# Another written-out order for the first stage of a fused attention, MLP and expert kernel

## Chip, cores, metric

One core of a Trainium2 chip. The metric is the time of one execution on the device in microseconds (us); the kernel before takes 545.9 us (median of three runs, 545.31 to 547.83).

## What is computed

Three layers follow each other on 1536 tokens (2 x 768) of width 512 (8 heads x 64). All inputs come as float64, are read by the kernel as pairs of 32-bit words, or, for q, k, v, as float32.

```python
scores = scale * np.matmul(q_c, k_full.transpose(0, 1, 3, 2))   # chunks of 32 queries, 64 keys
a = np.exp(scores - np.max(scores, axis=-1, keepdims=True))
out[:, :, c_start:c_end] = np.matmul(a / (np.sum(a, axis=-1, keepdims=True) + 1e-09), v_full)
...
h = x @ w_in                                                    # 512 -> 2048
g = np.where(h > 0.0, h, np.exp(np.minimum(h, 0.0)) - 1.0)
x = g @ w_out                                                   # 2048 -> 512
...
expert_idx = np.argmax(x @ w_gate, axis=1)                      # 8 experts, capacity 384
...
h = np.maximum(np.einsum('ecd,edf->ecf', disp, w1), 0.0)
y = np.einsum('ecf,efd->ecd', h, w2)
out[i] = gate_w[i] * y[expert_idx[i], pos[i]]
```

## The kernel before

The tokens are cut into six tiles of 256 (called tile or pair 0 to 5), the middle layer's 2048 columns into sixteen units of 128. A step is two (unit, tile) pairs. Steps 0 to 3 take units 0 to 3 on tiles 0 and 1, steps 4 to 15 one unit each on both tiles, steps 16 to 47 two units each on tiles 2 to 5. The first stage, steps 0 to 15 and what goes with them, is emitted from a table of words, `ORDER` (L33 to L36): `do` reads one word after the other and emits that piece, so the table is at once the order of TensorE's, VectorE's, ScalarE's, GpSimd's and the load queue's own instructions. [...] A word is two letters and an index:

- Loads on the queue of SyncE: `lk`, `lq`, `lv` for k, q, v of a tile's half (`lq01` is tile 0, half 1; 512 KB, 256 KB, 512 KB), `lu` for both weight halves of a unit (`lu10`: unit 10, 2 x 512 KB).
- Attention of a tile's half: `sc` scores (L170, TensorE), `tm` and `ts` their maximum (VectorE), `ex` the exponentials (eight ScalarE instructions with sums, or one), `to` the reciprocal of the sum (VectorE), `di` the division (GpSimd), `fl` four transposes (L239, TensorE), `fc` their copy (ScalarE), `av` the product with the values (L255, TensorE), `xh` its rounded part (L270, ScalarE), `xl` the remainder (L274, VectorE). Both make up the tile's `xt`.
- A unit's weights from words to floats: `ca` (L358, ScalarE), `cb`, `cc`, `cd` (L378, L382, L391, VectorE); then rounded part and remainder of the first half (`ch`, `cl`) and of the second (`dh`, `dl`): L403 on ScalarE and L407 on VectorE.
- A step: `ma` first product (L465, 24 matmuls), `mr` three ScalarE instructions (L479 to L481), `mv` two on VectorE (L485, L491), `mh` and `ml` rounded part and remainder (L495, L499), `mb` second product (L520). Steps 0 to 5 skip `mh` and `ml` and take the unrounded weights in `mb`.
- `pm`, a filler product on the identity matrix (L456), which computes nothing that is used.

A star puts a word's instruction on VectorE instead of ScalarE or GpSimd, a plus puts it on GpSimd instead of VectorE.

Buffers tie the queues. Nineteen buffers of 8 KB hold the units' raw words, the split weights and `xt`; the load of a later unit waits until an earlier unit's raw words are done with, which is after its `dl`. The two accumulators of `ma` alternate, so `ma` of a step waits for `mv` of the step two before. Six more PSUM buffers serve the rest.

From step 16 on a loop emits one step at a time: `ma` of two steps ahead, a piece of background work, `mr`, `mv`, `mh`, `ml` of that step, another piece, `mb`, a third piece. Which pieces stands in `PLANS` (L26 to L31), one row per tile from tile 2 on: 16 entries for 8 steps, where A is attention of the next tile, R and S routing of an earlier one; what stands behind the bar comes after `mr` to `ml` and ahead of `mb`. Routing of tiles 0 to 4 adds up eight gate values on VectorE (L552), takes the maximum (L584 to L590), and has TensorE count places (L595 to L601).

Of the kernel before, what the change touches and what calls it, by code (L numbers as in the profile page):

```python
# [30 lines left out]
)  # L31

ORDER = """  # L33
lq00 lk00 pm pm pm pm sc00 tm00 ts00 ex00 lu0 cb0 to00 ca0 lq01 cc0 lk01 pm pm pm pm pm sc01 tm01 ts01 lu1 ca1 di00 pm pm fl00 cd0 fc00 cb1 cc1 cd1 ex01 to01 lk10 lq10 lv00 pm sc10 av00 ch0 ch1 lu2 tm10 di01 cb2 lk11 xh00 xl00 ca2 pm pm fl01 fc01 lv01 pm pm av01 lq11 ts10 cl1+ cc2 cd2 lu3 ex10 lq20 to10 lk20 xh01 xl01 lv11 sc11 tm11 ts11 ch2 ca3 cb3 cc3 cl0+ pm ma0 lv10 lu4 sc20 lu5 lu6 di10 fl10 cl2+ ex11 to11 di11* cd3 ch3* tm20 pm pm pm fl11 fc10 pm av10 xh10* fc11 mr0 mv0 av11 xh11 xl11 lq21 cl3+ cb4 ca4 cc4 cd4 xl10 ma1 lu7 mb0 mr1 mv1 ch4 cl4+ ca6 cb6 cc6 cd6 ma2 mr2 mv2 lu8 ts20 ch6 cl6+ lk21 mb1 mb2 ma3 lu9 cb7 cb9 cb5 ca7 dh6 dl6 ex20 ca5 lu10 ca10 cc7 cd7 ca8 mr3 cc5 cd5 dh0* mv3 sc21 ma4 dl0+ to20 di20 mb3 ch5 cl5 cb8 dh1 dl1 mr4 ca9 cc9 mv4 ch7 dh2 dl2+ cb10 cl7 ma5 cd9 mr5 dh7 cc8 mv5 mb4 dh4 lu11 tm21 ca11 cd8 dl4 lu12 ca12 cc10 ma6 mr6 mv6 ch9 dh9 dh3 dl3 mh6 dl7+ mb5 dh5* lv20 cl9+ ts21 ex21 ml6+ ch8* dh8 to21 cl8+ lu13 dl8 ma7 mr7 mv7 mb6 ma8 fl20 ma9 dl5+ cb11 mh7 mr8 cd10 ch10 cb12 ml7 mb7 dl9 mv8 mh8 ml8+ mb8 cl10 ma10 cc11 cd11 mr9 mv9 lv21 lu14 dh10 dl10+ lu15 ca15 ch11 cl11 mh9 ml9 cc12 cd12 mb9 fc20 ma11 mr10 mv10 mh10 ml10 di21 mb10 fl21 ch12 dh12 cl12 ma12 dl12 cb13 dh11 dl11 ca13 cc13 cd13 mr11 mv11 ch13 cl13 fc21 mh11 ml11 ca14 cb14 cc14 av20 xh20 xl20 dh13 dl13+ mb11 cd14 ch14* mr12 dh14 mv12 mh12 ml12 cb15 cc15 av21 xh21 ma13 mr13 mv13 mh13 cl14+ ma14 xl21 mr14 dl14+ mb12 ml13 mb13 cd15 ch15* cl15+ mv14 mh14 ma15 ml14 mb14 dh15 dl15 mr15 mv15 mh15 ml15 ma16 mr16 mv16 mh16 ml16+ mb15 ma17 mr17 mv17 mh17 ml17 lw lz0 lz1 lz2 lz3 lz4 lz5 lz6 lz7 lz8 lz9 lz10 lz11
"""


# [1190 lines left out]
```

## Time and profile before

| | us |
|---|---|
| median of three runs | 545.9 |
| the profiled execution's own time | 546.62 |
| its span in the trace | 544.9 |
| TensorE busy | 522.4 |
| VectorE busy | 347.4 |
| ScalarE busy | 292.9 |
| GpSimd busy | 124.3 |

The span is the time from the first to the last instruction in the trace; the 1.7 us between it and the execution's time lie around it. TensorE has work in 96% of the span, and the other engines are well below that as a mean. The mean hides the first 120 us, in which all sixteen units are converted and split: there VectorE has work nine tenths of the time. TensorE's share also counts the fillers (42 records, two to a word, 14.0 us), all in the first 32 us.

### The profile page before, as it was taken

The page shows a single profiled execution, that of the slowest core. Times are in us where ns is not written, and L with a number is a line of the kernel's source. Part 1 is how long each engine was busy: PE and PEld are TensorE (multiplying, and loading weights), DVE is VectorE, ACT ScalarE, POOL GpSimd, SP SyncE. Part 2 cuts the span into 40 slices and gives each one's busy share as a digit, 9 for nine tenths or more (in the row PEclk, how much of TensorE's full clock was granted, in tenths as well). Part 3 has the DMA queues.
Part 4 walks back from the last instruction along what each step waited for, and adds up shares of the span by engine and source line. Part 5 has one row for each costly group of instructions (what it writes and reads, how often), then busy time and mean ns, then how long its engine had stood idle before and what let it go on. Part 6 is the DMA issues. An engine that isn't in the chain of part 4 may idle for free. (4 is left out here: it accounts for less than half of the span.)

```text
span 544.9 us, 11455 instructions
## 1 busy us (share of the span) xinstructions
PE 522.4 (96%) x4520; PEld 448.0 (82%) x4520; DVE 347.4 (64%) x651; ACT 292.9 (54%) x569; POOL 124.3 (23%) x140
## 2 busy tenths in 40 slices
PE   7899999999999999999999999999999998999995
PEld 5766678988998888998888997878887886889894
DVE  5888989984456333787766996442685764674550
ACT  3877776764546447444545356242665655654441
POOL 2411354031123313124312324221001011010101
PEclk9899999999999999999999999899999998999999
DMA  8994349994004305431004562529539929905000
GB/s 342 402 413 198 131 177 281 265 352 154 1 21 136 118 2 194 155 134 61 3 2 155 211 235 96 193 96 379 175 118 353 396 79 380 362 28 193 20 7 26
DMA packets 34726, 95.94 MB, mean 176 GB/s; under 512 B 3424, under 2 KB 3424, under 8 KB 33888
## 3 DMA queue, kind: packets, MB, share of 16 engines
q1 hardware_dynamic: 32496, 88.68, 45.9%
q0 software_dynamic: 2160, 6.31, 3.0%
q8 instruction: 46, 0.75, 0.6%
q14 instruction: 24, 0.20, 0.1%
HBM read 88.67 MB, written 16.55 MB: 193 GB/s over the span
## 5 line engine op out<-in xcount | busy, mean ns | idle before, releaser
L465 PE MATMUL hp<-xt,un 128*128 128x256 f32 x1152 | 149.7, 286 | 1.3 <-ACT xt L270 0.6
L465 PEld LDWEIGHTS hp<-xt,un 128*128 128x128 f32 x1152 | 142.9, 191 | 7.3 <-issue 2.4
L520 PE MATMUL ps<-un,gt 128*128 128x512 f32 x504 | 125.5, 397 | 1.4 <-POOL gt L499 1.3
L520 PEld LDWEIGHTS ps<-un,gt 128*128 128x128 f32 x504 | 91.6, 188 | 22.1 <-POOL gt L499 2.4
L707 DVE TENSOR_TENSOR eu<-eraw,eu 128x1024 fp32r<-128x1024 f32 x65 | 77.3, 1225 | 19.5 <-ACT eu L706 12.9
L830 PE MATMUL ps<-eu,ht 128*128 128x512 f32 x336 | 82.6, 398 | 1.0 <-DVE eu L707 0.8
L830 PEld LDWEIGHTS ps<-eu,ht 128*128 128x128 f32 x336 | 61.8, 188 | 15.2 <-DVE eu L707 1.6
L499 POOL TENSOR_TENSOR gt<-th,gt 128x512 fp32r<-128x512 f32 x33 | 45.8, 1387 | 124.5 <-ACT gt L495 124.5
L485 DVE SCALAR_TENSOR_TENSOR th<-e,th 128x512 f32<-128x512 f32 x48 | 34.6, 722 | 51.9 <-ACT e L481 51.7
L706 ACT CAST eu<-eraw 128x1024 fp32r<-128x1024 f32 x65 | 65.2, 1046 | 0.7 <-ACT os L836 0.7
L495 ACT CAST gt<-th 128x512 fp32r<-128x512 f32 x42 | 26.1, 620 | 73.5 <-DVE th L491 73.5
L767 PE MATMUL hp<-xd,eu 128*128 128x256 f32 x480 | 59.1, 284 | 3.0 <-DVE eu L707 2.1
L767 PEld LDWEIGHTS hp<-xd,eu 128*128 128x128 f32 x480 | 58.1, 192 | 4.4 <-DVE eu L707 2.5
L479 ACT ACTIVATE e<-hp 128x512 f32<-128x512 f32 x48 | 28.8, 600 | 36.5 <-PE hp L465 34.8
L837 POOL DMA_INDIRECT out_dram<-os,meta x14 | 13.8, 983 | 138.0 <-ACT os L836 133.4
L407 POOL TENSOR_TENSOR un<-raw,un 128x512 fp32r<-128x512 f32 x16 | 23.9, 1500 | 54.6 <-ACT un L403 38.3
L792 PE MATMUL hq<-eu,xd 128*128 128x512 f32 x120 | 33.4, 427 | 2.4 <-issue 2.0
L753 DVE SCALAR_TENSOR_TENSOR ht<-hp,ht 128x512 fp32r<-128x512 f32 x20 | 13.8, 689 | 33.3 <-ACT ht L752 33.3
L480 ACT ACTIVATE th<-e 128x512 f32<-128x512 f32 x48 | 30.4, 632 | 5.6 <-DVE junk L552 3.0
L491 DVE SCALAR_TENSOR_TENSOR th<-hp,th 128x512 f32<-128x512 f32 x42 | 29.0, 691 | 4.0 <-DVE th L485 0.5
L481 ACT ACTIVATE e<-e 128x512 f32<-128x512 f32 x48 | 30.4, 632 | 1.5
L836 ACT ACTIVATE os<-ps,meta 128x512 f32<-128x512 f32 x14 | 9.6, 688 | 38.8 <-PE ps L830 28.5
(157 smaller groups left out, 594.0 us busy)
## 6 DMA issues: line engine op xcount, KB each, us to landing
eraw<-in_moe_w_dram SPq DMA_DIRECT2D x32, 1024.0 KB, 7.6
raw<-in_moe_w_in_dram SPq DMA_DIRECT2D x15, 512.0 KB, 7.6
raw<-in_moe_w_out_dram SPq DMA_DIRECT2D x15, 512.0 KB, 8.2
disp<-in_blank_dram SPq DMA_DIRECT2D x12, 514.0 KB, 14.8
kt<-in_k_dram SPq DMA_DIRECT2D x12, 512.0 KB, 6.8
v<-in_v_dram SPq DMA_DIRECT2D x12, 512.0 KB, 5.4
wb<-in_gate_rows_dram SPq DMA_DIRECT2D x6, 1024.0 KB, 4.6
xg<-disp SPq DMA_DIRECT2D x8, 514.0 KB, 9.5
```

The costliest lines, as they stand in the source:

```text
L465: nc.tensor.matmul(hp[:, j, :], units[f].un[:, 0, wp, kk * P : (kk + 1) * P], xts[ti][:, xp, kk, :], start=(n == 0), stop=(n == 3 * KD - 1),)
L480: nc.scalar.activation(th, e, AF.Tanh, scale=0.5)
L481: nc.scalar.activation(e, e, AF.Exp, scale=-1.0)
L485: nc.vector.scalar_tensor_tensor(out=th, in0=e, scalar=1.0, in1=th, op0=ALU.add, op1=ALU.mult)
L491: nc.vector.scalar_tensor_tensor(out=to, in0=hv, scalar=0.0, in1=th0, op0=ALU.max, op1=ALU.subtract)
L499: eng.tensor_tensor(out=gt[:, 1, :], in0=th, in1=f32(gt[:, 0, :]), op=ALU.subtract)
L520: nc.tensor.matmul(accs[ti][bl], x, w, start=(f == 0 and n == 0), stop=(f == NF - 1 and n == len(passes) - 1),)
L706: nc.scalar.copy(un[:, 0, :], raw)
L707: lows.tensor_tensor(out=un[:, 1, :], in0=raw, in1=f32(un[:, 0, :]), op=ALU.subtract)
L767: nc.tensor.matmul(hp[:, j, :], w1p(kk, wp, f * P, P), xd[xp][:, kk, :], start=(n == 0), stop=(n == 3 * KD - 1),)
L792: nc.tensor.matmul(hp, self.xd[xp][:, kk, self.b0 * P : (self.b0 + 1) * P], w1p(kk, wp, i * 512, 512), start=(n == 0), stop=(n == 3 * KD - 1),
L830: nc.tensor.matmul(acc, hof(f, gp, j), w2p(f, wp), start=(f == 0 and n == 0), stop=(f == NFE - 1 and n == 2))
```

## The change

The table `ORDER` is written anew; the words are the same 356, 21 fillers among them, but 34 of them change their engine, and nearly all their place in the order. Two rows of `PLANS` move a piece of attention and four pieces of routing. The program is otherwise the same.

```diff
 PLANS = (
-    "RR - A|S R RS SAA - RAA S SAA - A| - - - -",
-    "A A A ARA - ARAR RR| - |AR - - R RR R RR| R",
+    "RR - A|S R RS SAA - RAA S SAA |A - - - - -",
+    "A A A ARA - ARAR RR| - |AR R R R R - RR| R",
...
-lq00 lk00 pm pm pm pm sc00 tm00 ts00 ex00 lu0 cb0 to00 ca0 lq01 cc0 lk01 pm pm pm pm pm sc01
...
+lk00 lq00 pm pm pm pm sc00 tm00 ts00 ex00 lu0 lq01 cb0 to00 lk01 ca0 cc0 cd0 pm pm pm pm pm pm sc01
...
```

By word, the engines change so: VectorE gets one more `cl`, three more `dl`, three `fc` and one `di`, and gives up two `ch` and two `ml`, four instructions more in all. GpSimd loses one `di`, one `cl`, three `dl` and gets two `ml`. ScalarE loses three `fc` and gets two `ch`.

TensorE from the last filler ahead of the first product (`hp_112`, step 0) on, before; `ps_525` and `ps_554` are the transposes of tile 1, `gt_607` is step 0 after `mv`:

```order
L456 MATMUL hp_112<-ident 128x256
L465 MATMUL hp_112<-xt_283,un_318 128x256 x12
L465 MATMUL hp_112<-xt_283,un_320 128x256 x12
...
L239 MATMUL ps_525<-ident,a_391 128x128 x4
L456 MATMUL hp_550<-ident 128x256 x3
L239 MATMUL ps_554<-ident,a_531 128x128 x4
L456 MATMUL hp_550<-ident 128x256
...
L465 MATMUL hp_550<-xt_283,un_449 128x256 x12
L465 MATMUL hp_550<-xt_283,un_545 128x256 x12
L520 MATMUL ps_682<-raw_158,gt_607 128x512
```

And with the change:

```order
L456 MATMUL hp_112<-ident 128x256
L239 MATMUL ps_449<-ident,a_299 128x128 x4
L465 MATMUL hp_112<-xt_314,un_269 128x256 x12
L465 MATMUL hp_112<-xt_314,un_441 128x256 x12
L239 MATMUL ps_502<-ident,a_485 128x128 x4
...
L520 MATMUL ps_612<-raw_158,gt_552 128x512
...
L465 MATMUL hp_626<-xt_314,un_549 128x256 x12
L465 MATMUL hp_626<-xt_314,un_555 128x256 x12
L465 MATMUL hp_658<-xt_507,un_269 128x256 x12
```

Between `ma0` and `mb0` stand now one transpose group and the two values products (left out here as "..."), and neither a filler nor `ma1`; the four fillers that stood there are ahead of `ma0`, and `ma1` and `ma2` come after `mb0`.

VectorE with the change, around `mv5` (`gt_909`), `mv6` (`hp_913`) and `ml6` (`gt_960`); `raw_455` is unit 3, `raw_941` unit 10, `raw_949` unit 11:

```order
L407 TENSOR_TENSOR un_555<-raw_455,un_555 128x512
L485 SCALAR_TENSOR_TENSOR th_887<-e_886,th_887 128x512
L491 SCALAR_TENSOR_TENSOR gt_909<-hp_861,th_887 128x512
L407 TENSOR_TENSOR un_893<-raw_618,un_893 128x512 x2
L378 TENSOR_SCALAR raw_941<-raw_941 128x1024
L407 TENSOR_TENSOR un_895<-raw_621,un_895 128x512
L485 SCALAR_TENSOR_TENSOR th_954<-e_953,th_954 128x512
L491 SCALAR_TENSOR_TENSOR th_954<-hp_913,th_954 128x512
L378 TENSOR_SCALAR raw_949<-raw_949 128x1024
L407 TENSOR_TENSOR un_725<-raw_597,un_725 128x512
L499 TENSOR_TENSOR gt_960<-th_954,gt_960 128x512
```

Units 10 and 11 are loaded into buffers that earlier units leave: unit 10's load waits for VectorE, TensorE and ScalarE, unit 11's for VectorE, TensorE and GpSimd, and the last `dl` on VectorE ahead of them in the table is the first row here, `dl3`, and `dl7`, the second of the two `un_893`. Before, unit 10 still had a buffer of its own, and the first load that waited was unit 11's. The conversion of the two new units (`raw_941`, `raw_949`) stands ahead of `mv6` and `ml6`.

VectorE in tile 3, the routing of tile 2 (`lg_2636`), before and with the change; `hp_2893`, `hp_2943` and `hp_2896`, `hp_2949` are the accumulators of two steps in a row:

```order
L485 SCALAR_TENSOR_TENSOR th_2919<-e_2918,th_2919 128x512
L491 SCALAR_TENSOR_TENSOR th_2919<-hp_2893,th_2919 128x512
L552 SCALAR_TENSOR_TENSOR junk_2940,lg_2636<-x_268_2431,wb_2780 128x512
...
L485 SCALAR_TENSOR_TENSOR th_2975<-e_2974,th_2975 128x512
L491 SCALAR_TENSOR_TENSOR th_2975<-hp_2943,th_2975 128x512
L584 MAX rmx_2996<-lg_2636 128x8 x2
L586 MAX_INDEX rix_2997<-rmx_2996,lg_2636 128x8 x2
...
L590 TENSOR_SCALAR oh_2999<-iota_e,idf_2998 128x8 x2
```

```order
L485 SCALAR_TENSOR_TENSOR th_2925<-e_2924,th_2925 128x512
L491 SCALAR_TENSOR_TENSOR th_2925<-hp_2896,th_2925 128x512
L552 SCALAR_TENSOR_TENSOR junk_2946,lg_2636<-x_268_2431,wb_2780 128x512
...
L584 MAX rmx_2974<-lg_2636 128x8 x2
L586 MAX_INDEX rix_2975<-rmx_2974,lg_2636 128x8 x2
...
L590 TENSOR_SCALAR oh_2977<-iota_e,idf_2976 128x8 x2
L485 SCALAR_TENSOR_TENSOR th_2992<-e_2991,th_2992 128x512
L491 SCALAR_TENSOR_TENSOR th_2992<-hp_2949,th_2992 128x512
```

Four of the eight gate-value instructions that stood between the two `mv` have moved ahead of the first, and the maximum and the one-hot rows (`oh`) ahead of the second.

## Rows read from the trace of the kernel before

**Rows 1.** The page: span, busy time and instructions of each engine.

```profile
span 544.9 us, 11455 instructions
PE 522.4 (96%) x4520; PEld 448.0 (82%) x4520; DVE 347.4 (64%) x651; ACT 292.9 (54%) x569; POOL 124.3 (23%) x140
```

**Rows 2.** Busy time by stretch: length, engines (instructions), granted clock, DMA share, GB/s.

```profile
0.00:24.20 24.20, 18.95 (x426) 14.74 (x426) 15.08 (x28) 13.08 (x45) 7.29 (x16) 0.93 0.95 373
24.20:40.90 16.70, 15.46 (x267) 12.23 (x265) 14.86 (x27) 11.74 (x32) 4.01 (x4) 1.00 1.02 405
40.90:71.60 30.70, 30.57 (x218) 21.21 (x217) 28.00 (x37) 22.35 (x44) 8.75 (x6) 1.00 0.46 173
71.60:140.00 68.40, 67.28 (x531) 58.37 (x530) 54.88 (x77) 41.69 (x71) 17.57 (x14) 1.00 0.76 232
```

**Rows 3.** Timeline of TensorE: start, length, instructions, idle before and its releaser.

```profile
24.76 3.02 PE L465 MATMUL hp<-xt,un 128*128 128x256 f32 x23 [0.16 <-DVE xt L274]
27.71 0.86 PE L170 MATMUL ps<-kt,q 64*32 64x64 f32 x64
...
28.99 1.46 PE L456 MATMUL hp<-ident 128*128 128x256 f32 x6
...
33.77 1.02 PE L255 MATMUL ps<-at,v 64*64 64x32 f32 x56 [0.64 <-issue]
34.72 3.14 PE L465 MATMUL hp<-xt,un 128*128 128x256 f32 x24
37.70 3.77 PE L520 MATMUL ps<-raw,gt 128*128 128x512 f32 x8
40.87 3.46 PE L465 MATMUL hp<-xt,un 128*128 128x256 f32 x24
44.17 7.56 PE L520 MATMUL ps<-raw,gt 128*128 128x512 f32 x16
```

**Rows 4.** Timeline of the load queue, and issue to landing of single loads.

```profile
11.18 0.43 SPq L141 DMA_DIRECT2D v<-in_v_dram  x1
...
v<-in_v_dram SPq DMA_DIRECT2D x1, 512.0 KB, 10.2
...
raw<-in_moe_w_out_dram SPq DMA_DIRECT2D x1, 512.0 KB, 4.4
```

**Rows 5.** Timeline of ScalarE and VectorE around `mr2` and `mv2`.

```profile
44.37 0.60 ACT L479 ACTIVATE e<-hp 128x512 f32<-128x512 f32 x1 [2.89 <-PE hp L465]
...
46.32 0.69 DVE L485 SCALAR_TENSOR_TENSOR th<-e,th 128x512 f32<-128x512 f32 x1 [1.05 <-ACT e L481]
47.12 0.69 DVE L491 SCALAR_TENSOR_TENSOR gt<-hp,th 128x512 f32<-128x512 f32 x1
```

**Rows 6.** Busy time by stretch again, for the granted clock (the column after POOL).

```profile
8.00:16.00 8.00, 4.86 (x143) 3.36 (x141) 7.67 (x13) 5.21 (x19) 1.84 (x1) 1.00 1.03 416
16.00:22.00 6.00, 5.46 (x96) 4.58 (x99) 4.42 (x10) 4.34 (x14) 4.00 (x3) 0.72 1.03 414
...
30.00:34.00 4.00, 2.92 (x97) 2.11 (x96) 3.70 (x9) 2.35 (x4) 1.29 (x1) 1.00 1.03 413
```

**Rows 7.** Groups of 0 to 140 us: busy us, mean ns of one, idle before.

```profile
L407 DVE TENSOR_TENSOR un<-raw,un 128x512 fp32r<-128x512 f32 x14 | 10.5, 759 | 0.2 <-ACT un L403 0.2
...
L407 POOL TENSOR_TENSOR un<-raw,un 128x512 fp32r<-128x512 f32 x16 | 23.9, 1500 | 54.6 <-ACT un L403 38.3 <-DVE un L403 14.9 <-PE hp L465 1.4
```

**Rows 8.** Waits of TensorE between 34.7 and 140 us: us, times, longest.

```profile
PE ps L520 <- POOL gt L499: 0.7, 1, 0.7
```

**Rows 9.** Timeline at the end of tile 2.

```profile
184.41 0.62 ACT L495 CAST gt<-th 128x512 fp32r<-128x512 f32 x1 [1.55 <-DVE th L491]
184.94 0.64 ACT L270 CAST xt<-ps 128x256 fp32r<-128x256 f32 x2
...
185.36 3.47 PE L465 MATMUL hp<-xt,un 128*128 128x256 f32 x24 [0.59 <-ACT xt L270]
```

**Rows 10.** Timeline of TensorE in tile 3, the counting of places.

```profile
245.98 0.17 PE L598 MATMUL ps<-oh,stri 128*128 128x8 bf16 x1 [0.89 <-DVE oh L590]
```

More of the change, by code (lines that the diff above doesn't have):

```diff
@@ L33 @@
 ORDER = """
-lq00 lk00 pm pm pm pm sc00 tm00 ts00 ex00 lu0 cb0 to00 ca0 lq01 cc0 lk01 pm pm pm pm pm sc01 tm01 ts01 lu1 ca1 di00 pm pm fl00 cd0 fc00 cb1 cc1 cd1 ex01 to01 lk10 lq10 lv00 pm sc10 av00 ch0 ch1 lu2 tm10 di01 cb2 lk11 xh00 xl00 ca2 pm pm fl01 fc01 lv01 pm pm av01 lq11 ts10 cl1+ cc2 cd2 lu3 ex10 lq20 to10 lk20 xh01 xl01 lv11 sc11 tm11 ts11 ch2 ca3 cb3 cc3 cl0+ pm ma0 lv10 lu4 sc20 lu5 lu6 di10 fl10 cl2+ ex11 to11 di11* cd3 ch3* tm20 pm pm pm fl11 fc10 pm av10 xh10* fc11 mr0 mv0 av11 xh11 xl11 lq21 cl3+ cb4 ca4 cc4 cd4 xl10 ma1 lu7 mb0 mr1 mv1 ch4 cl4+ ca6 cb6 cc6 cd6 ma2 mr2 mv2 lu8 ts20 ch6 cl6+ lk21 mb1 mb2 ma3 lu9 cb7 cb9 cb5 ca7 dh6 dl6 ex20 ca5 lu10 ca10 cc7 cd7 ca8 mr3 cc5 cd5 dh0* mv3 sc21 ma4 dl0+ to20 di20 mb3 ch5 cl5 cb8 dh1 dl1 mr4 ca9 cc9 mv4 ch7 dh2 dl2+ cb10 cl7 ma5 cd9 mr5 dh7 cc8 mv5 mb4 dh4 lu11 tm21 ca11 cd8 dl4 lu12 ca12 cc10 ma6 mr6 mv6 ch9 dh9 dh3 dl3 mh6 dl7+ mb5 dh5* lv20 cl9+ ts21 ex21 ml6+ ch8* dh8 to21 cl8+ lu13 dl8 ma7 mr7 mv7 mb6 ma8 fl20 ma9 dl5+ cb11 mh7 mr8 cd10 ch10 cb12 ml7 mb7 dl9 mv8 mh8 ml8+ mb8 cl10 ma10 cc11 cd11 mr9 mv9 lv21 lu14 dh10 dl10+ lu15 ca15 ch11 cl11 mh9 ml9 cc12 cd12 mb9 fc20 ma11 mr10 mv10 mh10 ml10 di21 mb10 fl21 ch12 dh12 cl12 ma12 dl12 cb13 dh11 dl11 ca13 cc13 cd13 mr11 mv11 ch13 cl13 fc21 mh11 ml11 ca14 cb14 cc14 av20 xh20 xl20 dh13 dl13+ mb11 cd14 ch14* mr12 dh14 mv12 mh12 ml12 cb15 cc15 av21 xh21 ma13 mr13 mv13 mh13 cl14+ ma14 xl21 mr14 dl14+ mb12 ml13 mb13 cd15 ch15* cl15+ mv14 mh14 ma15 ml14 mb14 dh15 dl15 mr15 mv15 mh15 ml15 ma16 mr16 mv16 mh16 ml16+ mb15 ma17 mr17 mv17 mh17 ml17 lw lz0 lz1 lz2 lz3 lz4 lz5 lz6 lz7 lz8 lz9 lz10 lz11
@@ new lines @@
+lk00 lq00 pm pm pm pm sc00 tm00 ts00 ex00 lu0 lq01 cb0 to00 lk01 ca0 cc0 cd0 pm pm pm pm pm pm sc01 tm01 ts01 di00 lu1 cb1 ca1 cc1 lq10 lk10 pm pm pm pm pm pm sc10 tm10 ch0 cl0+ ex01 to01 di01 ts10 lu2 ca2 fl00 fc00* lv00 ex10 cb2 pm pm pm pm av00 cd1 cc2 fl01 fc01 lk11 lq11 to10 di10 lv01 sc11 tm11 xh00 av01 ts11 xl00 ch1 xh01 xl01 cd2 pm fl10 lq20 lu3 cb3 cl1+ lv10 ma0 ex11 fc10 to11 di11* ca3 cc3 fl11 av10 fc11* mr0 ch2 mv0 cd3 ch3 cl3+ cl2 lv11 av11 xh11 lk20 lu4 lu5 xh10* xl10 cb4 cb5 lu6 mb0 lu7 lu8 ca4 ca6 ma1 mr1 xl11 ma2 mr2 sc20 cc4 cb6 cd4 ch4 lu9 ca9 mv1 mb1 cc6 cd6 ca8 mv2 ca5 ch6 dh6 ma3 mr3 tm20 ts20 cb8 cc8 cd8 cc5 mb2 dh0 cd5 cb9 ch5 cl4+ ma4 mv3 mb3 cl5 cb7 cc9 ca7 cc7 dl0 ex20 to20 mr4 lk21 mv4 dh2 dh1 dl1 ma5 mr5 dl2 cd7 ch7* ch8 dh8 cd9 ch9* dh3 dl3 dh7 mb4 mv5 dh4 cl6+ ma6 dl6+ cl7 dl7 lu10 cb10 mb5 lu11 cl8 mr6 ca10 mv6 mh6 dh5 cb11 ma7 dl4 ml6 mb6 cc10 ca11 dh9 cd10 mr7 ch10 dh10 mv7 lv21 lu12 mh7 dl5 ml7 ca12 ma8 di20 mb7 cb12 cl10 cc12 cd12 mr8 mv8 cl9+ cc11 cd11 dl10 ma9 mh8 ml8 lu13 mr9 mv9 ch11 dh11* cl11 lv20 cb13 dl8+ dl9+ ma10 mr10 mb8 mh9 lq21 ca13 ma11 mv10 mh10 ml9+ mb9 mr11 ch12 dh12 sc21 ml10 mb10 lu14 lu15 ca14 ca15 cb14 cc13 cd13 dl11 tm21 ts21 ch13 mv11 mh11 cl13 cl12+ ma12 dl12 ex21 to21 fl20 dh13* dl13 cc14 mr12 ml11+ mb11 fc20 av20 cd14 ch14 dh14 mv12 ma13 di21* xh20 xl20 fl21 fc21* cl14+ ma14 dl14+ mh12 ml12 mr13 mr14 cb15 cc15 cd15 ch15 cl15+ mv13 av21 xh21 mh13 ml13+ dh15 mb12 xl21 mv14 dl15 mh14 ml14+ ma15 mr15 mb13 mb14 mv15 mh15 ml15 mb15 ma16 mr16 mv16 ma17 mh16 mr17 ml16 mv17 mh17 ml17+ lw lz0 lz1 lz2 lz3 lz4 lz5 lz6 lz7 lz8 lz9 lz10 lz11
```

## The prediction

> **What bounds the kernel now.** I read the page first: TensorE has work in 522.4 of 544.9 us, every other engine in 64% or less [rows 1]. So the time is TensorE's own queue, and only what makes that queue wait, or what it computes without need, can be won. The table of stretches says where that is [rows 2]. In the first 24.2 us TensorE is idle for 5.3 us and its clock is below full; in the next 16.7 us it is idle for 1.2; from 40.9 to 140 us for 0.13 and 1.12. The 14.0 us of filler lie in the first two stretches and count as busy. In the second and third stretch VectorE is busy for 14.9 of 16.7 and 28.0 of 30.7 us: it feeds TensorE, and one more instruction there can become a wait. The reader is to see that the order in the first 45 us decides how soon TensorE's dense part begins, and that after it there is hardly a wait left to remove, but much to spoil.
>
> **The start up to `ma0`.** `ma0` needs both halves of tile 0 attended, so it can't begin before the last values load (`lv01`) has landed: issued at 11.18, landed 10.2 later, 21.4 [rows 4]. With the change 7.0 MB of loads stand up to and with it, before 6.75; at the 405 GB/s of that stretch [rows 2] the 0.25 MB more are 0.6 us, so 22.0. Behind it come the values product, `xh` and `xl`. Before, the first full product resumed at 24.76 [rows 3], 3.4 us behind the load, though there the load was no longer what it waited for. I take 24.6 with the change, a gain of 0.2, bounds a loss of 1.0 and a gain of 0.5. The fillers are all ahead of it now, 17 of them behind `sc00`, where TensorE would wait for loads anyway: they cost nothing there, and if a load came earlier, half a microsecond each.
>
> **From `ma0` to `mb1`.** Before: `ma0` resumed at 24.76, `mb1` started at 44.17 [rows 3], with `ma1`, `mb0`, `ma2`, the transposes, two values products and `sc20` between, and besides them eight filler records (six of them 1.46 us) and waits, 0.64 the longest [rows 3]. `ma1` had to wait for tile 1's attention, and `mb0`, which needs only what follows `ma0`, came behind it. With the change `mb0` is next after the values products. What it needs is `mr0` and `mv0`. The same chain took from 44.37 to 47.81, 3.44 us, in step 2 [rows 5]. `ma0` ends at 24.6 + 2.95 (24.76 to 27.71 before), so `mb0` starts at 31.0; the two `av` (56 of their 128 records took 1.02 [rows 3], so 2.3 in all) and the transposes fit ahead of it, the second `av` if `fc11`, now on VectorE behind `cc3`, is done by 29.6. From there `mb0` takes 3.17 (37.70 to 40.87), `ma2` behind another product as much as `ma1` did, 2.98 (34.72 to 37.70), `ma1` behind `mb0` 3.30 (40.87 to 44.17), `sc20` 0.86 or a little less (27.71): `mb1` could start at 41.25. Its `mv1` is due 3.44 behind `ma1`'s end at 37.5, and ScalarE has unit 6's `ca` ahead of `mr1`, for which I add half a microsecond: 41.4. That is 44.17 - 41.4 = **2.8 us gained**. It becomes 3.4 if `mv0` and `mv1` meet no queue, and 0.8 if ScalarE and VectorE each reach `mr0` and `mv0` a microsecond late.
>
> [...]
>
> **From `mb1` to `mb6`.** Before, `mb1` and `mb2` ran as one block from 44.17 to 51.15, 7.0 us for twice 3.17 [rows 3]: `mb2` waited inside it for `mv2`, done at 47.81 [rows 5]. With the change `ma3` stands between. Gain 0.6, bounds 0 and 0.7. Against it, VectorE has four instructions more in the stage, 4 x 0.76 = 3.0 us, and GpSimd three fewer, 4.5 us [rows 7]. VectorE was busy for 28.0 of 30.7 us here, with waits of its own (1.05 before `mv2` [rows 5]) that take up part of it.
>
> **The loads of units 10 and 11.** Their buffers come free on VectorE, at the latest with `dl3`, whose `dh3` follows `mr5` and two casts on ScalarE. `ma5` ends at 41.4 + 3 x (3.17 + 3.30) = 60.8. With 1.95 for `mr5` (44.37 to 46.32 [rows 5]), 0.53 for each of three casts [rows 9] and 0.76 for `dl3` [rows 7] that is 65.1. A unit's second half landed 4.4 us after its issue [rows 4], which is 0.4 behind the first half's: unit 10 at 69.9, unit 11 one more megabyte later (1.05 MB at 405 GB/s, 2.6 us) at 72.5. Behind that on VectorE come `cb11`, `dl4` and `ml6`, 2.3 us, to 74.8. TensorE is at `mb6` at 60.8 + 2 x (3.17 + 3.30) = 73.7. I charge **1.0 us lost**, bounds 0 (an earlier buffer) and 2.6 (both late by a unit's transfer).
>
> **The rest of the stage.** One wait of 0.65 (0.7 in the table) for GpSimd's remainder was before [rows 8]; its counterparts on VectorE are due just in time. Gain 0.5, bounds 0 and 1.1. At the end `ma16`, `ma17` and `ma18` now follow each other with no `mb` between, so `ma18` waits for `mv16`: 3.44 of chain against 2.98 of `ma17`: **0.4 lost**, bounds 0 and 0.6.
>
> **The two rows of `PLANS`.** At the end of tile 2 the values product moves ahead of `mb`. The next product waited for `xh`, on ScalarE at 184.94, right behind `mh` at 184.41 [rows 9]; ScalarE's order is the same, so `xh` runs at 184.94 again, and the 0.59 stay: nothing, bound 0.6 if `xh` was held by the product after all. In tile 3 TensorE waited 0.89 for the one-hot rows [rows 10]; they now stand ahead of an `mv` and four gate values earlier, two to three us of VectorE, and the `mv` that they pass are due a step later: **0.9 gained**, bounds 0 and 0.9.
>
> **Sum.** 0.2 + 2.8 + 0.6 - 1.0 + 0.5 - 0.4 + 0.9 = 3.6 us. At about eight places of the stage a product's input is due less than half a microsecond ahead of it, by durations that are means; I take 0.3 off for their scatter. 3.3 us against the profiled 546.62 are 543.3; that execution stands 0.7 above the median 545.9, so the forecast is **542.6**, its own range 540.4 to 543.9. A difference under 0.5%, 2.7 us, can hardly be told from none, so 543.2 and 548.6 are the edges.
>
> **Rivals.** *What the start wins is given back at VectorE.* For it: the three us more on it, where it is nine tenths busy. Against: it had 5 us of waits up to 72 us. TensorE then reaches the stage's end 3.0 later than I say, and of 3.6 us 0.6 stay: 545.3. *Slower:* unit loads at VectorE's head. `cb10`, `cb11` and `cb12` stand ahead of `mv6`, `ml6` and `mv8`, and each buffer is freed by a `dl` behind such a wait, so a late load delays the next load's issue. If `dl3` comes over 2 us later than 65.1, each of three loads costs a transfer of 2.6 us: 7.8 - 3.6 = 4.2 lost, 550.1. For it: the slack at `mb6` is nil. Against: before, unit 11's load was waited for in the same way, and no product waited. *The clock falls behind `ma0`:* 0.28 of 6 us [rows 6], 1.7 lost of what the forecast wins: 544.3. [...]
>
> **Chances.** Forecast 0.55, given back 0.22, slower 0.12, clock 0.11. Of the first about 0.4 lie under 543.2, of given back 0.02 and of the clock 0.04: faster 0.46, slower 0.12, same 0.42. The range is 540.4 to 547.2: it takes in all cases but the slower one and the outer part of the second.
>
> **What would show it.** Right: `mb0` ahead of `ma1` at 30.5 to 32 and `mb1` at 41 to 42.5; no filler behind `ma0`; at `mb6` a wait below 1 us, released by VectorE; at tile 3 no wait at L598; at tile 2's end still a wait for `xh`. Wrong: `ma0` after 26; waits of VectorE for a `raw` load of over 2 us together with waits of TensorE for `gt`; a clock under 1.00 between 25 and 40; a stage as dense as before that ends no earlier.

## The result, and the profile after

The changed kernel takes 549.62 us (median of 20 runs, 547.11 to 552.4) against 546.47 for the kernel before (20 runs, 543.76 to 549.52): ratio 1.0063, 95% interval 1.0045 to 1.0081. It is slower by 0.6%; 542.6 was forecast, with a range of 540.4 to 547.2. The profiled execution took 551.4 us, 1.8 above its kernel's median, so some 1.6 us of the 4.8 that the two traces differ by at their ends belong to the two executions and not to the kernels.

The page of the changed kernel, to set against [rows 1]: TensorE computes as long as before (522.4 there), VectorE 5.5 us longer (347.4).

```profile
span 549.7 us, 11462 instructions
PE 522.2 (95%) x4520; PEld 449.5 (82%) x4520; DVE 352.9 (64%) x655; ACT 293.0 (53%) x568; POOL 122.7 (22%) x137
```

Busy time by stretch, the columns as in [rows 2]:

```profile
0.00:24.20 24.20, 17.88 (x347) 13.87 (x348) 15.15 (x27) 12.21 (x42) 7.45 (x17) 1.00 0.93 365
24.20:40.90 16.70, 14.39 (x256) 11.52 (x256) 12.39 (x24) 9.24 (x28) 2.05 (x2) 0.80 0.79 302
40.90:71.60 30.70, 28.64 (x215) 20.61 (x214) 28.89 (x37) 21.28 (x44) 6.91 (x4) 1.00 0.28 111
71.60:140.00 68.40, 67.42 (x579) 57.55 (x578) 59.34 (x83) 43.71 (x72) 17.14 (x13) 1.00 0.85 272
```

In the second stretch every engine works less than before (VectorE 12.39 us for 14.86, ScalarE 9.24 for 11.74), the loads too (302 GB/s for 405), and the clock is 0.80: something held all of them up. In the third TensorE is idle for 2.06 us where it was for 0.13, and VectorE is busier than before.

TensorE's timeline around `ma0` (against [rows 3]) shows the first of the two:

```profile
16.39 0.30 PE L170 MATMUL ps<-kt,q 64*32 64x64 f32 x2 [0.87 <-issue]
...
21.34 0.66 PE L170 MATMUL ps<-kt,q 64*32 64x64 f32 x43
25.39 0.64 PE L170 MATMUL ps<-kt,q 64*32 64x64 f32 x21 [3.38 <-issue]
25.96 1.93 PE L255 MATMUL ps<-at,v 64*64 64x32 f32 x64
...
29.54 4.02 PE L465 MATMUL hp<-xt,un 128*128 128x256 f32 x24
...
37.11 3.84 PE L520 MATMUL ps<-raw,gt 128*128 128x512 f32 x8 [1.12 <-DVE gt L491]
```

In the middle of `sc11`, behind 43 of its 64 products, TensorE stops for 3.38 us. Its operands have been there since before the first product (k landed at 20.5 and q at 21.2, and the products start at 21.34), and no semaphore ends the gap (the releaser is given as "issue": nothing that the profile shows). All that hangs on `sc11`, `av01` and `ma0` stops with it, and the granted clock is 0.50 from 24.75 to 31.58. Four stretches show it, with the granted clock behind POOL's column:

```profile
16.00:22.00 6.00, 5.11 (x125) 4.10 (x126) 5.97 (x10) 4.81 (x26) 1.16 (x2) 1.00 1.03 416
22.00:25.40 3.40, 0.02 (x4) 0.01 (x2) 0.47 (x3) 1.19 (x4) 2.29 (x2) 0.91 0.90 359
25.40:32.00 6.60, 6.60 (x104) 6.08 (x104) 4.94 (x12) 4.06 (x20) 0.00 (x0) 0.53 0.49 155
32.00:36.00 4.00, 3.99 (x145) 3.71 (x144) 2.58 (x4) 2.84 (x5) 0.00 (x0) 1.00 1.03 418
```

The reading that the experiments below test is that TensorE lacked instructions. The DMA queues by stretch (packets, MB, share) list only the loads from 15 to 22.9 us, and one packet of the instruction queue, 16 KB, in the next 1.2 us. It starts at 23.00 and takes 0.99 us, and TensorE goes on 1.4 us behind its end. First 22.9 to 24.1 us of the changed kernel:

```profile
q1 hardware_dynamic: 130, 0.47, 97.4%
q8 instruction: 1, 0.02, 5.2%
```

In the kernel before the same packet starts at 20.30 (20.2 to 21.3 us):

```profile
q1 hardware_dynamic: 120, 0.43, 98.1%
q8 instruction: 1, 0.02, 5.3%
```

Counted over all that is recorded of TensorE (products, weight loads and its sequencer's instructions), the gap stands ahead of the 706th instruction, and the smaller one at 16.39 (behind 62 of 64 products of `sc10`) ahead of the 450th: 256 apart. The kernel before has such a gap too. The 0.64 us that [rows 3] show ahead of 33.77, behind 72 of 128 values products, stands ahead of its 1218th instruction, 512 further on, and ends 1.3 us behind the end of a packet that starts at 31.40 and takes 1.08. No view says what a packet holds or which engine it is for; that TensorE waits for it is inferred from these distances and times.

The second loss is in the third stretch. The waits of TensorE from 25 to 146 us (us, times, longest):

```profile
PE ps L520 <- DVE gt L491: 3.7, 3, 2.1
PE ps L170 <- issue: 3.4, 1, 3.4
PE hp L465 <- DVE th L491: 0.8, 1, 0.8
PE ps L520 <- POOL gt L499: 0.5, 1, 0.5
```

`mb0` waits 1.12 us (above), `mb3` 2.06 and `mb5` 0.50 for a value from VectorE. `mb6`, where the prediction had its wait, has none. These three on TensorE's timeline:

```profile
62.69 3.87 PE L520 MATMUL ps<-raw,gt 128*128 128x512 f32 x8 [2.06 <-DVE gt L491]
...
76.39 3.87 PE L520 MATMUL ps<-raw,gt 128*128 128x512 f32 x8 [0.50 <-DVE gt L491]
...
82.96 2.96 PE L520 MATMUL ps<-un,gt 128*128 128x512 f32 x12
```

VectorE's timeline ahead of `mv3` (61.15 and 61.94), and GpSimd's beside it:

```profile
53.05 0.70 DVE L378 TENSOR_SCALAR raw<-raw 128x1024 int32<-128x1024 int32 x1
53.86 2.14 DVE L382 SCALAR_TENSOR_TENSOR raw<-raw 128x1024 int32<-128x1024 int32 x1
56.03 2.21 DVE L391 SCALAR_TENSOR_TENSOR raw<-raw 128x1024 int32<-128x1024 int32 x1
58.16 1.21 DVE L382 SCALAR_TENSOR_TENSOR raw<-raw 128x1024 int32<-128x1024 int32 x1
59.41 1.23 DVE L391 SCALAR_TENSOR_TENSOR raw<-raw 128x1024 int32<-128x1024 int32 x1
60.55 0.69 DVE L378 TENSOR_SCALAR raw<-raw 128x1024 int32<-128x1024 int32 x1
61.15 0.69 DVE L485 SCALAR_TENSOR_TENSOR th<-e,th 128x512 f32<-128x512 f32 x1
61.94 0.69 DVE L491 SCALAR_TENSOR_TENSOR gt<-hp,th 128x512 f32<-128x512 f32 x1
```

```profile
53.16 4.00 POOL L407 TENSOR_TENSOR un<-raw,un 128x512 fp32r<-128x512 f32 x2 [2.23 <-ACT un L403]
```

No idle time stands in VectorE's rows; it works through the conversion of units 8, 5 and 9 ahead of `mv3`, and two of these instructions take 2.14 and 2.21 us instead of 1.22 while GpSimd computes two remainders. Up to `ma18` VectorE (the third busy time) works 4.4 us longer than before, with four instructions more; first the kernel before, then the changed one:

```profile
0.00:139.94 139.94, 132.19 (x1435) 106.49 (x1435) 112.82 (x167) 88.85 (x190) 37.56 (x39) 0.99 0.76 264
0.00:145.89 145.89, 133.44 (x1434) 108.44 (x1434) 117.24 (x171) 88.33 (x189) 33.55 (x35) 0.98 0.72 253
```

The milestones (start on TensorE, us; `ma0` before is the start of its dense part, as in the prediction, and 137.5 adds up the prediction's terms up to there):

| | before | forecast | after | after - before |
|---|---|---|---|---|
| `ma0` | 24.76 | 24.6 | 29.54 | 4.8 |
| `mb1` | 44.17 | 41.4 | 47.42 | 3.3 |
| `ma18` (end of the stage) | 139.94 | 137.5 | 145.89 | 6.0 |
| product behind tile 2's `xh` | 185.36 | | 191.40 | 6.0 |
| product behind tile 3's counting | 248.94 | | 254.01 | 5.1 |
| end of the span | 544.92 | | 549.70 | 4.8 |

### The profile page after: what moved, and what is told of

It is laid out like the page before. It is cut to its first block, busy times and chain, and to the rows that moved or that the text cites. A ratio compares the mean times of both kernels' runs of the same rounds, so it can differ in the third digit from the quotient of the medians.

```text
span 549.7 us, 11462 instructions
## 1 busy us (share of the span) xinstructions
PE 522.2 (95%) x4520; PEld 449.5 (82%) x4520; DVE 352.9 (64%) x655; ACT 293.0 (53%) x568; POOL 122.7 (22%) x137
## 5 line engine op out<-in xcount | busy, mean ns | idle before, releaser
L499 POOL TENSOR_TENSOR gt<-th,gt 128x512 fp32r<-128x512 f32 x35 | 48.8, 1396 | 142.8 <-ACT gt L495 139.1
L485 DVE SCALAR_TENSOR_TENSOR th<-e,th 128x512 f32<-128x512 f32 x48 | 38.3, 797 | 53.4 <-ACT e L481 51.7
L792 PE MATMUL hq<-eu,xd 128*128 128x512 f32 x120 | 31.2, 405 | 3.5 <-ACT eu L706 2.3
L407 POOL TENSOR_TENSOR un<-raw,un 128x512 fp32r<-128x512 f32 x12 | 18.9, 1586 | 47.9 <-ACT un L403 47.9
```

The lines of the kernel that those rows point to most:

```text
L485: nc.vector.scalar_tensor_tensor(out=th, in0=e, scalar=1.0, in1=th, op0=ALU.add, op1=ALU.mult)
L499: eng.tensor_tensor(out=gt[:, 1, :], in0=th, in1=f32(gt[:, 0, :]), op=ALU.subtract)
L792: nc.tensor.matmul(hp, self.xd[xp][:, kk, self.b0 * P : (self.b0 + 1) * P], w1p(kk, wp, i * 512, 512), start=(n == 0), stop=(n == 3 * KD - 1),
```

## The experiments

Ratios are to the kernel before, run on the same chip, with the 95% interval in brackets. `ORDER` is one long line, of which the diffs show the part that changed. The theory called CODE is the late packet. FULL says that VectorE has no slack in the new order, and its rival HEAD that only the order ahead of `mv3` is at fault. SHARED says that VectorE's instructions become longer where GpSimd works beside them.

**The same kernel again; ORDER alone; PLANS alone.** The first is unedited; the second is the changed kernel with the two old rows of `PLANS`, the third the kernel before with the two new ones.

> The changed kernel once more. Theory CODE: TensorE's instructions come in packets of 16 KB on the instruction queue; in the changed kernel the packet that holds what stands behind TensorE's 706th recorded instruction starts only at 23.0 us, behind the loads issued at 16.7 to 17.6, and TensorE stands still inside the scores of tile 1 (43 of 64 records done) from 22.0 to 25.4. Then the gap is there again, at the same record to within one or two, 2.5 to 4 us long, the granted clock is 0.5 behind it, and ma0 resumes at 28.5 to 30. Rival CHANCE: the gap was an accident of one execution; then it is gone or elsewhere, and ma0 resumes near 25. Time against the kernel before: 1.003 to 1.009.

> The new ORDER with the old two rows of PLANS. What the two traces show of PLANS is 0 at the end of tile 2 and 1.0 us won in tile 3 (TensorE was 6.09 late before it and 5.07 behind). Theory PLANS-IS-ONE: 1.0 us slower than the changed kernel, 4 us slower than before (ratio 1.006 to 1.011), and the wait of 0.9 for the one-hot rows in tile 3 is back. Rival PLANS-IS-MORE: something of the loss came from PLANS; then it is not slower than the changed kernel.

> The old ORDER with the two new rows of PLANS. Theory PLANS-IS-ONE: 1.0 us faster than before (ratio 0.997 to 0.999), the first stage as before (ma0 resumes at 24.7 to 24.9, one stretch of 3.4 us at half clock), no wait for the one-hot rows. Rival: the same as before to 0.3 us, if the microsecond won is given back at the end of tile 3 or in what follows.

Measured: 1.0055 (1.0029 to 1.0082), 1.0052 (1.0026 to 1.0078), 0.9985 (0.9964 to 1.0006). The gap is there again in the first two, behind the same 43 products, 3.40 and 3.39 us long, so it was no accident of one execution. In the second TensorE waits 0.9 for the one-hot rows again; it is 5.1 us late against before on both sides of them, the changed kernel 6.1 and then 5.1. So `PLANS` wins the 1.0 us, in the trace. The times are too wide to show it: the second was expected to be slower than the first, and their medians are 548.89 and 549.61. The third was run a second time:

> The old ORDER with the new rows of PLANS once more, to narrow its interval of 0.9964 to 1.0006: 0.998 to 0.999 of before if the 1.0 us won in tile 3 stays; 1.000 if it is given back in the later stages.

0.9984 (0.9952 to 1.0016). Both intervals reach 1.000; both ratios are about 0.15% below it. With the old order the 706th instruction falls into `av01`; in the third kernel TensorE stops there too, behind 53 of 64 products, but briefly:

```profile
21.51 1.00 PE L255 MATMUL ps<-at,v 64*64 64x32 f32 x53 [1.14 <-DMA v<-in_v_dram]
22.82 0.42 PE L255 MATMUL ps<-at,v 64*64 64x32 f32 x11 [0.30 <-issue]
```

**Does the gap go by count?**

```diff
-lq10 lk10 pm pm pm pm pm pm sc10
+lq10 lk10 sc10
```

> The changed kernel without the six fillers ahead of sc10: 24 recorded instructions fewer on TensorE (12 products with their weight loads). Theory CODE: the gap comes at the same count of TensorE's instructions, so 24 records later in the program: behind the 55th of the 64 products of tile 1's second scores instead of the 43rd, still ending 1.4 us behind the end of an instruction packet. The gap at the 450th record, behind the 62nd product of sc10, leaves sc10 altogether. Rival PLACE: something about sc11 itself (its operands, its bank) holds it; then the gap stays behind the 43rd.

```profile
22.73 0.78 PE L170 MATMUL ps<-kt,q 64*32 64x64 f32 x55
25.27 0.32 PE L170 MATMUL ps<-kt,q 64*32 64x64 f32 x9 [1.76 <-issue]
```

With 24 recorded instructions fewer ahead of it, the gap stands 12 products later, behind the 55th, and ends 1.5 us behind the end of a packet: CODE, and not the place. (One execution of 554.63 us; its time is not read.)

**What makes the packet late?** First the loads issued at 16.7 to 17.6, just behind the 450th instruction (16.39):

```diff
-fl10 lq20 lu3 cb3 cl1+ lv10 ma0
+fl10 lv10 lq20 lu3 cb3 cl1+ ma0
```

> The changed kernel with the loads of tile 2's first queries and of unit 3 (1.25 MB, issued at 16.7 to 17.6) moved behind the first values load of tile 1 (issued at 20.7). Theory CODE with its packet queued behind those loads: the packet starts 3 us earlier, near 20.0, the gap inside tile 1's scores shrinks from 3.4 us to under 0.7, ma0 resumes at 25 to 26.5, at most one stretch of 3.4 us at half clock, and the time falls by 3.5 to 5 us against the changed kernel (0.997 to 1.000 of before). Rival CODE-BY-COUNT: the packet's delay hangs on how many instructions TensorE has issued and not on the loads; then the gap stays within 0.5 us of 3.4 and the time is that of the changed kernel or up to a microsecond worse.

The packet starts at 20.28, the gap is 0.65 us, `ma0` starts at 25.60, as CODE said. But the time is 1.009 (1.0052 to 1.0129), slower than CODE's forecast: `cb3` now stands at VectorE's head for a load that lands late, and `di11` behind it. Behind that wait `mb0` takes 5.51 us for 3.84; the mean granted clock of the execution is 0.982, where the first run above has 0.993. VectorE's row, and TensorE's behind it:

```profile
30.03 0.70 DVE L378 TENSOR_SCALAR raw<-raw 128x1024 int32<-128x1024 int32 x1 [2.83 <-DMA raw<-in_moe_w_out_dram]
```

```profile
31.92 0.63 PE L239 MATMUL ps<-ident,a 128*128 128x128 f32 x4 [3.11 <-DVE a L233]
```

So the conversion of unit 3 was moved as well, behind `mv0` and `xl10`:

```diff
-fl10 lq20 lu3 cb3 cl1+ lv10 ma0 ex11 fc10 to11 di11* ca3 cc3 fl11
+fl10 cl1+ lv10 lq20 lu3 ma0 ex11 fc10 to11 di11* fl11
...
-mr0 ch2 mv0 cd3 ch3 cl3+ cl2 lv11 av11 xh11 lk20 lu4 lu5 xh10* xl10 cb4 cb5
+mr0 ch2 mv0 cl2 lv11 av11 xh11 lk20 lu4 lu5 xh10* xl10 cb3 ca3 cc3 cd3 ch3 cl3+ cb4 cb5
```

> The kernel with the two loads moved, and now the conversion of unit 3 (cb3, ca3, cc3, cd3 and what hangs on it) moved too, behind mv0 and tile 1's transposed values, so that no engine waits at its head for that load. Theory CODE, with the wait of 3.1 us of the run before as a second, separate fault (VectorE's head held by a load): the gap inside tile 1's scores stays under 0.8 us, ma0 resumes at 25.3 to 26, TensorE waits under 1 us for the one-over-sum product ahead of fl11, mb0 starts at 31.5 to 33.5 instead of 37.1, and the time is 3.5 to 5.5 us under the changed kernel's (0.996 to 1.000 of before). Rival SHIFTED: what is saved at the start is waited for again by mb3, since VectorE's work up to mv3 is the same; then mb3 waits 4 us or more and ma18 starts less than 1.5 us earlier than the 145.9 of the changed kernel.

The gap is 0.93 us. `ma0` starts at 25.66 and `mb0` at 32.37, as expected; `ma18` at 143.41, 2.5 us earlier than in the changed kernel, where 3.9 were won at `ma0`. The time is 1.0050 (1.0025 to 1.0075), short of what was expected. `ma1` waits 0.55 and 1.12 for unit 3's cast and remainder, which the edit itself made late; behind that its last products and `ma2`, 34 in all, take 5.83 us for 4.33 in e7 below. The granted clock is 0.93 as a mean from 25.66 to 49.64, and 1.00 from 25.58 to 48.05 in e7. `mb3` (0.69) and `mb5` (0.50) still wait for VectorE. SHIFTED, which wanted 4 us at `mb3`, falls. Then the load the other way:

```diff
-to10 di10 lv01 sc11
+to10 di10 lu3 lv01 sc11
```

> [...]

Both halves of unit 3 are now issued ahead of the 450th instruction (13.12 and 13.76, for 17.09 and 17.56 in the changed kernel). The gap is 3.40 us again; the packet starts at 23.35, 6.8 behind the 450th instruction. So unit 3's load just behind that instruction is not what makes it late here. The depth of the queue could be, but other executions speak against both. All profiled ones, in us, counted from the 450th instruction, 256 ahead of the 706th:

| kernels | 450th instruction | packet starts | between | gap at the 706th |
|---|---|---|---|---|
| changed, again (e1), ORDER alone (e2), `mv3` (e6), old engines (e11), load earlier (e13) | 15.8 to 16.6 | 22.6 to 23.4 | 6.5 to 6.9 | 2.6 to 3.4 |
| loads later: e4, e5, e7 | 15.8 to 16.0 | 20.3 to 20.5 | 4.3 to 4.6 | 0.7 to 1.2 |
| without signs: e9, e14 | 16.7, 16.1 | 20.1, 19.6 | 3.4 | 0.3, 0.0 |
| six fillers fewer: e8 | 19.3 | 22.8 | 3.5 | 1.8 |
| old ORDER, six executions | 16.7 to 17.2 | 20.3 to 20.8 | 3.6 | up to 0.3 |

(In the old ORDER the 1218th instruction has the longer gap, 0.43 to 1.25 us.) The two without signs (below) issue the very same loads in the same places, and differ from the changed kernel only behind 40 us; their packet comes in 3.4 us, both times. The chip doesn't decide it: e9 and e11 ran on one, e13 and e14 on another. So as far as these executions show it is the program that decides, reproducibly; by what stays open.

**Is VectorE's order or its sum the fault at `mb3`?**

```diff
-cb8 cc8 cd8 cc5 mb2 dh0 cd5 cb9 ch5 cl4+ ma4 mv3 mb3 cl5 cb7
+cb8 cc8 cd8 mv3 cc5 mb2 dh0 cd5 ch5 cl4+ ma4 mb3 cl5 cb9 cb7
```

> The changed kernel with mv3 moved ahead of cc5, cd5 and cb9 on VectorE (cb9 goes behind cl5). Theory HEAD: mb3's wait of 2.06 us is VectorE's order, with cc5, cd5 and cb9 (3.2 us) ahead of mv3; the wait goes to under 0.4 us, ma18 starts 1 to 2 us earlier, the gap in tile 1's scores and ma0 stay as they are, and the time falls by 1 to 2 us (0.996 to 0.998 of the changed kernel). Rival FULL: VectorE has no slack, so what mb3 no longer waits for, ma5 (unit 5's remainder) or mb4 waits for; then ma18 moves by less than 0.5 us.

`mb3` no longer waits, and `mb4` waits 2.46 instead:

```profile
61.97 3.45 PE L465 MATMUL hp<-xt,un 128*128 128x256 f32 x24
67.88 5.37 PE L520 MATMUL ps<-raw,gt 128*128 128x512 f32 x8 [2.46 <-DVE gt L491]
```

From `ma0` to `ma18` it takes 116.7 us, the changed kernel 116.4; the time is 1.0096 (1.006 to 1.0132). The wait moved: for `mb3`'s 2.06 and `mb5`'s 0.50 stands one of 2.46, and behind it `mb4` takes 5.37 us; `mb3` took 3.87 behind its wait, at a granted clock of 1.00. FULL holds, HEAD falls. All moves together (with `mb15` back between `ma16` and `ma17`):

> The two moves above together (the loads with their conversion, and mv3), and mb15 put between ma16 and ma17 as in the kernel before, so that ma18 needn't wait for mv16 (0.8 us). If the causes add: 3.5 to 5.5, 1 to 2 and 0.5 to 0.8 us under the changed kernel, 5 to 8 in all, so 0.991 to 0.997 of before. If VectorE is full (rival FULL), 4 to 5 us and mostly from the start: 0.997 to 1.000.

1.0049 (1.0013 to 1.0085): the wait ahead of `ma18` is gone, `mb4` waits 2.42 and `mb5` 0.91, here at a granted clock of 1.00 (48.05 to 83.87 us), with `mb4` in 3.87. The gains don't add up. The test of VectorE's sum itself, on the new order and on the old: the kernel leaves out `cd`, the sign, of units 4 to 9.

```diff
             for lw, hw in zip(self.lows(), self.highs()):
+                if 4 <= self.f <= 9:
+                    continue
                 nc.vector.scalar_tensor_tensor(
                     out=lw, in0=hw, scalar=-(1 << 31), in1=lw, op0=ALU.bitwise_and, op1=ALU.bitwise_or
```

> The changed kernel with the sign instruction (cd) of units 4 to 9 left out: six instructions fewer on VectorE, 7.3 us at 1.22 each, and the weights of those units lose their sign. Theory FULL: from mb1 to ma9 TensorE waits for VectorE's sum of work and not for one badly placed instruction; then the waits ahead of mb3 (2.06 us) and mb6 (0.50) fall under 0.3 us each, ma18 starts 2 to 3.5 us earlier than 145.9, and the time is 0.993 to 0.997 of the changed kernel's. The gap in tile 1's scores stays. Rival LOADS: mb3 and mb6 wait for unit loads or for ScalarE's mr; then they still wait 1.5 us or more together.

> The kernel before with the same six sign instructions left out, as the control: if its order hides VectorE's work, ma18 stays within 0.6 us of its 139.9 and the time within 0.998 to 1.001. If VectorE bounds the kernel before as well, ma18 comes 1 us or more earlier.

Without their signs the weights send tokens to other experts (TensorE has 4228 products for 4520), so the total times (0.9825 and 0.9809) say nothing, which the expectations overlooked; the first stage can be read. The new order: `ma18` at 137.83 (145.89), and `ma0` to `ma18` 112.0 us for 116.4. The waits ahead of `mb3` and `mb5` (which the expectation calls `mb6`) are gone; the gap, expected to stay, is 0.29. The old order: `ma18` at 140.02 (139.94). There `ma1` is 0.84 later, behind a gap of 1.25 (0.64 before) ahead of the 1218th instruction, and 0.76 is won behind it. So from `ma1` to `ma18`, where the granted clock is 1.00 in the kernel before and in the changed one, the same six instructions are worth 3.8 us in the new order (101.7 for 105.5) and 0.8 in the old (104.5 for 105.2). Once more, for the gap:

> The kernel without the signs of units 4 to 9 once more. In its first execution with a profile the gap was 0.3 us, although the same loads were issued 0.3 to 1.15 us behind the 450th record as in the changed kernel, whose gap was 3.4 in three of three. If chance decides, the gap can be 3 us here and ma0 at 28 to 30, and ma0 to ma18 stays 112.0 us (to 0.9 more with half clock in ma0): VectorE's part is then read apart from the gap. If something in that program decides, the gap is under 0.5 us again and ma18 starts at 137.5 to 138.5.

No gap inside `sc11`: `ma0` at 24.41, `ma18` at 137.06, 112.7 apart, and again 101.7 from `ma1` on.

```profile
21.18 1.10 PE L170 MATMUL ps<-kt,q 64*32 64x64 f32 x64
...
24.41 3.11 PE L468 MATMUL hp<-xt,un 128*128 128x256 f32 x24
...
31.54 2.94 PE L523 MATMUL ps<-raw,gt 128*128 128x512 f32 x6 [0.35 <-DVE gt L494]
```

(Lines behind 400 stand three higher in this kernel.)

**The engines.** The changed kernel with all 34 words on their old engines:

> The changed kernel with all 34 words back on the engines of the kernel before, the order as changed. VectorE has four instructions (3.0 us) fewer, GpSimd three more. Theory FULL by count: ma18 starts 1 to 3 us earlier than 145.9 (as far as the 3 us lie ahead of mb6), time 0.995 to 0.998 of the changed kernel's. Rival SHARED: VectorE's instructions take up to 1 us longer where GpSimd runs its remainder beside them (2.14 and 2.21 against 1.22 us at 54 to 58 us), so that what VectorE hands over comes back as longer instructions; then ma18 comes within 0.7 us of 145.9 or later. The gap of 3.4 us stays in both.

1.0249 (1.0202 to 1.0296), `ma18` 13 us later than in the changed kernel, with waits for ScalarE (3.1), VectorE's remainders (2.2, 1.7) and `gt` (3.5). Handing VectorE's work to GpSimd doesn't relieve VectorE here. Up to `ma18` it is busy for 117.58 us with 167 instructions, for 117.24 in the changed kernel with 171, and for 112.82 in the kernel before, also with 167: what was handed over came back as longer instructions, as SHARED expects. That this alone makes the 13 us is not shown, since heads of queues changed too and the mean granted clock is 0.981 (0.988 in the changed kernel).

**A try at a faster kernel.** The old `ORDER`, the new `PLANS`, and two marks:

```diff
-ml8+
+ml8
...
-cl15+
+cl15
```

> The old ORDER with the two new rows of PLANS, and ml8 and cl15 on VectorE instead of GpSimd, for which TensorE waited 0.65 and 0.47 us in the kernel before. If PLANS gives its 1.0 us and both waits go without VectorE being late elsewhere, ma18 starts 0.8 to 1.1 us earlier than 139.9 and the time is 1.8 to 2.1 us under the kernel before (0.996 to 0.997). If VectorE is late for it, ma18 moves by less than 0.4 us and the ratio is that of the rows of PLANS alone, 0.998 to 0.999.

> The old ORDER with the new rows of PLANS and ml8 alone on VectorE. The kernel with ml8 and cl15 there stood still for 6.1 us at 410.5 (record 7646 of TensorE), ended 1.4 us behind the end of an instruction packet, as its six times all say (550.7 to 555.2). If the two marks themselves cost that, half or all of it is here: 547 to 553. If it is where the packets of the engines fall in the stretch in which the experts' weights are loaded, then this program need not meet it, the 0.65 us are won, and the time is 0.996 to 0.998 of before.

1.0122 (1.008 to 1.0164) and 1.0116 (1.0077 to 1.0156), though at 400 us TensorE is ahead of the kernel before, by 2.5 and 0.8 us. The waits named are gone, both in the first kernel and `ml8`'s in the second. Then, among the experts, with the weights' loads filling the queue (DMA share 0.99 from 410 to 416.1 us), the same kind of gap, here of the kernel with `ml8` alone:

```profile
406.38 5.83 PE L830 MATMUL ps<-eu,ht 128*128 128x512 f32 x24
418.61 3.78 PE L792 MATMUL hq<-eu,xd 128*128 128x512 f32 x8 [6.40 <-issue]
```

A packet of the instruction queue starts at 416.2, and TensorE goes on 1.4 us behind its end; with both marks the gap is 6.14 at the same instruction. The kernel with `PLANS` alone waits 1.1 there, in both its profiles, for ScalarE. Behind the gap the 18 products of this group take 6.21 us for 4.37; with both marks the granted clock is 0.50 there (416 to 420 us). Gap and longer products together are 7.1 us more than with `PLANS` alone; the medians differ by 7.2 (553.05 and 545.86). So `ml8`, moved from one engine to another at 88 us, costs 1.2% by way of a packet 320 us later.

## Why the prediction was wrong

At `ma18` the forecast was missed by 145.89 - 137.5 = 8.4 us: 4.9 up to `ma0`, 3.5 from there. (The sum counts 0.2 twice: 41.4 for `mb1` is worked out from `ma0` at 24.6, so the 2.8 holds the 0.2 of the start already.) Two steps failed: that TensorE would have its instructions up to `ma0`, and that VectorE's longer sum would cost nothing but a wait for loads.

*The start up to `ma0`* failed: +0.2 was forecast, -4.8 measured. Its loads came nearly as said (the last values load at 22.4, for 22.0), but the step took for granted that TensorE has its instructions. 256 short ones are issued in 5.4 us (16.39 to 21.8), faster than the next packet came. The gap is 3.4 us; the rest is work at a granted clock of 0.50 (`av01` 1.93 us for 1.14, and what stands beside it). The prediction had one such gap in hand, the 0.64 of [rows 3], and read it as a wait like others. "They cost nothing there" leaves out that fillers are instructions: with their weight loads 80 of the 705 ahead of the gap. What that costs is not shown; with six fewer `ma0` came 2.1 us earlier, in one execution. Why the packet starts so late stays open.

*From `ma0` to `mb1`*: 16.8 us forecast, 17.88 measured; 0.9 of the difference is `ma0` at a mean granted clock of 0.74 (4.02 for 3.11). Against before (19.41) the step wins 1.5, not 2.8. In the four executions with `ma0` in 3.11 to 3.20 us (ORDER alone, six fillers fewer, and twice without signs) it takes 17.0 to 18.0, which wins 1.4 to 2.4. So the mechanism was right, with `mb0` next behind the values products and no filler there, and the term too large.

*From `mb1` to `mb6`* failed: VectorE's three us more were seen and charged only at the loads; 4.4 were measured. `mb2`'s wait went (+0.6 as forecast), and `mb3`'s 2.06 and `mb5`'s 0.50 came. Leaving out six instructions of VectorE shortens `ma1` to `ma18` by 3.8 us in the new order and by 0.8 in the old. So the rival "given back at VectorE", priced at 3.0, is what happened in this stretch.

*The loads of units 10 and 11* failed too: a loss of 1.0 at `mb6` was forecast, and `mb6` doesn't wait. The loads landed at 74.5 and 78.5, and VectorE came to them only at 77.77 and 80.36; it waited for no load between 40 and 84 us. The 0.50 stands at `mb5`, for `mv5`, which VectorE computes ahead of both units. The slower rival (late loads at VectorE's head) did not occur; that its 550.1 lies near the measured 549.62 is chance.

*The rest of the stage*: `mb8`'s wait for GpSimd (0.65) went, another of 0.47 came at `mb11`, the one for unit 15's remainder (0.47) went: near the 0.5. `ma18` waits 0.79 for `mv16`, 0.4 was forecast.

*`PLANS`*: right. At the end of tile 2 TensorE still waits for `xh`, and lateness stays 6.0; in tile 3 the 0.9 is gone and 1.0 is won.

```profile
191.40 3.47 PE L465 MATMUL hp<-xt,un 128*128 128x256 f32 x24 [0.42 <-ACT xt L270]
...
251.05 0.17 PE L598 MATMUL ps<-oh,stri 128*128 128x8 bf16 x1
```

*The clock behind `ma0`* was a rival at 0.11. It fell ahead of `ma0`, at 24.75, with work in 0.02 of the 3.40 us from 22.00 to 25.40, and was back at 1.00 from 31.58 on, ahead of `mb0`. In the kernel without signs, where `mb0` follows `ma0` as forecast, with no filler between (work in 10.01 of 11.60 us from 24.4 on), `ma1` and `ma2` take 6.34 us in both executions, for 6.33 in the changed kernel at 1.00. So no loss by the clock behind `ma0` shows, and the forecast has no term for one.

In the kernel without signs the packet is in time and VectorE is relieved, and the second execution comes close to the forecast: `ma0` 24.41, `mb1` 42.41, `ma18` 137.06, against 24.6, 41.4 and 137.5. It bears out TensorE's part of the sum, but as a whole it is in part luck: it does six instructions less, and its `mb1` is 1.0 late.

## What to carry to other kernels

Where TensorE issues some 250 short instructions within a few us beside a full load queue (here 256 in 5.4 us, at a DMA share of 1.03), look for gaps that "issue" ends in the middle of a group, and for the instruction queue's packet ahead of their end. Fillers and small products count there: six fillers fewer, 24 recorded instructions, moved the gap by 12 products. An order that gains by packing TensorE must be costed as a sum on the engine that feeds it: if that engine is hardly idle (here 28.89 of 30.70 us busy), a wait that is moved can come back at the next product (2.06 at `mb3`, then 2.46 at `mb4`), and taking work away from it as an experiment tells a full engine from a bad order.

## What the hardware showed unexpectedly

The 16 KB packet that TensorE seems to wait for takes 0.93 to 1.09 us once it moves, but starts 3.4 to 6.9 us behind the 450th instruction, beside the loads; where TensorE stops, it goes on 1.3 to 1.5 us behind the packet's end. The gap repeats (3.38 and 3.40 in two executions of one program, 3.39 in one with other `PLANS`), and goes with an edit that touches neither TensorE nor the loads at that place (0.3 and 0.0). Two of VectorE's conversion instructions take 2.14 and 2.21 instead of 1.22 us while GpSimd computes remainders beside them, and on the old engines 167 instructions make 112.82 us of VectorE's time up to `ma18` in the old order and 117.58 in the new.
